# The first K product in two parts, the last combines spread over three engines, and other constants for the order of work

## The chip, the cores and the metric

One core of one Trainium2 chip. The metric is the device time in microseconds (us). A span (the time on the core itself, without what comes before and after) was shorter than the time of the same run (705.4 us of span went with 707.33 us).

## The reference, cut to what matters

```python
x = A_x                                       # 1 x 2048 x 512, bf16
g = sigmoid((x * gate_w).sum(-1, keepdims=True))
a = softmax(q k^T * 16**-0.5) v @ wo          # 32 heads of 16, q, k, v = x @ wqkv
b = ((x @ w_gate) * (x @ w_up)) @ w_down      # 512 -> 1376 -> 512
out = g * a + (1 - g) * b
```

## The kernel before

The program is a list of instructions that a small scheduler in the kernel file makes before anything runs. It keeps one clock for each engine with estimated durations, and always lets the engine whose clock is lowest take its next step. What comes out is a fixed order for each engine; on the chip the engines only wait on semaphores. So a changed constant gives another order for all that follows.

The score tiles (128 keys x 512 queries) go to two engines. ScalarE evaluates the exponential for 1508 tiles, two or three at a time. VectorE and GpSimd take the others through an integer form. The tensor engine fills the rest of its time with "fillers": the q, k, v, gate, up and down products, in `start_fill` and `do_fill`. A run of up to four score tiles takes one row group of the array for each tile, all at once. A pack is four matmuls of a filler or of the PV product (the exponentials times v) that go side by side in four column groups (four of the kernel before start together at 24.58 us and take 0.39). A bank is a 128 x 512 f32 piece of psS, psX or psO, the kernel's PSUM tensors, to which the tensor engine's results go.

The start, cut: the first 512 tokens of x are transposed, then Q and K of the first head group are made.

```python
def evac(bk, last):                       # of a K filler
    dst = KE[:, b, ch * 512 : (ch + 1) * 512]
    if b == ch == 0:                      # the first K product: two copies on ScalarE
        ev_k[0, 0, 0] = add("act", [last], lambda a: a.activation(dst[:, 0:128], bk.ap[:, 0:128], ACT.Copy), ...)
        ev_k[b, ch]   = add("act", [last], lambda a: a.activation(dst[:, 128:512], bk.ap[:, 128:512], ACT.Copy), ...)
        return
    ev_k[b, ch] = add("dve", [last], lambda v: v.tensor_copy(dst, bk.ap), 0.6, prio=2, ...)
# ...
for f, bk in ((f_q(0, 0, 0), slots[1][2]), (f_k(0, 0, 0), slots[0][2])):
    fills.append(f)
    start_fill(f, bk)
    # ...
    while st["fill"] is not None:
        do_fill(clock["pe"])
```

The x of the other three quarters comes by transposing loads, four each, all on SyncE's queue:

```python
for ch in range(1, NCH):
    for kt in range(KD):
        o = load("sp", xT[:, kt, ch * 512 : (ch + 1) * 512], x2[...], f"dx{ch}", 1.31, 3.5, transpose=True)
    d_x.append(o)
```

The tail, cut: the denominators of the last heads go through Ln and Exp on ScalarE by 128 tokens, VectorE multiplies, the tensor engine makes the last part of the output product, and VectorE combines `g * a + (1 - g) * b`.

```python
for tt in range(4):
    a1 = now("act", [dens[tt], free], ... ACT.Ln ...)
    a2 = now("act", [a1], ... ACT.Exp, scale=-1.0 ...)
    if tt == 2:
        fin(0)                                  # combine of tokens 0..127, then its store
    mt = now("dve", [a2] + ..., ... psO[:, cs] * rlast[:, cs] ...)
    oo.append(pe_tail([mt], last_pack, PACK, 0.44))
for tt in range(1, 4):
    fin(tt)
```

The softmax here doesn't subtract the row's maximum and nothing guards it: scores larger than these inputs give would overflow.

## Time and profile before

| | |
|---|---|
| Time, median of the first three runs | 707.34 us (706.64 to 708.81) |
| Span of the profiled run | 705.4 us |
| Busy: PE, ScalarE, VectorE, GpSimd | 682.9, 691.7, 651.9, 499.6 us |
| Exponentials on ScalarE | 670: 500 of two banks, 169 of three, 1 of one |
| First exponential, end of the last | 9.56, 696.11 us |

A row in order of time reads: start, duration, engine, line, operation, output<-input, shapes, count, and in brackets the idle time of the engine before it with what ended it. When rows are merged, the duration is from the start of the first to the end of the last. The prediction below shows the lines.

### The profile page before, as it was taken

To read this page: it belongs to the slowest core of one execution; us is meant where nothing else is said; L and a number is where in the kernel's file an instruction comes from. 1 tells how busy PE (TensorE), PEld (TensorE's weight loads), DVE (VectorE), ACT (ScalarE), POOL (GpSimd) and SP (SyncE) were. 2 spreads that over 40 slices of the span, in tenths; PEclk is the share of its full clock that TensorE was granted. 3 is DMA by queue.
4 is the path that set the end of the run, shared out by engine and by line. 5 is a ranking of instruction groups with operands and counts; after the bars stand their busy time and mean duration, and the time that the engine had idled before them with its cause. 6 is when DMAs were issued, how large, how long until landed. Compare 5 with 4: busy or idle time off the path is not lost.

```text
span 705.4 us, 21702 instructions
## 1 busy us (share of the span) xinstructions
PE 682.9 (97%) x9299; PEld 193.8 (27%) x9299; DVE 651.9 (92%) x1223; ACT 691.7 (98%) x685; POOL 499.6 (71%) x515
## 2 busy tenths in 40 slices
PE   8999999999999999999999999999999999999997
PEld 3323332222222222222222222222222222222222
DVE  5999999999999999999998999999999999998897
ACT  6999999999999999999999999999999999999995
POOL 4777786678867756678788756668888676664873
PEclk9999999999999999999999999999999999999999
DMA  7700001000300001000000011000000010000001
GB/s 142 260 13 8 21 18 22 18 17 7 98 21 17 18 12 36 29 17 18 20 3 27 18 34 35 18 7 16 21 18 18 13 34 28 17 19 20 3 21 46
DMA packets 33056, 21.67 MB, mean 31 GB/s; under 512 B 20380, under 2 KB 27964, under 8 KB 32960
## 3 DMA queue, kind: packets, MB, share of 16 engines
q1 hardware_dynamic: 31632, 19.64, 9.7%
q8 instruction: 72, 1.18, 0.7%
q10 hardware_dynamic: 1328, 0.66, 0.4%
q14 instruction: 24, 0.20, 0.1%
HBM read 15.12 MB, written 2.36 MB: 25 GB/s over the span
## 4 chain that ended last, share of the span: by engine, by line
ACT 71%; PE 22%; DVE 4%; issue 2%; POOL 0%; DVEq 0%; ACTq 0%; POOLq 0%
ACT PT L1744 55%; PE psS L503 7%; ACT xT L1744 7%; PE psO L1245 6%; ACT wv L1744 5%; PE psX L582 5%; ACT wd L1744 2%; ACT hT L1744 2%; PE psS L582 1%; PE psX L503 1%; DVE PT L1102 1%; PE psS L693 1%; PE psX L693 1%; PE psO L1852 0%; DVE PT L1180 0%
## 5 line engine op out<-in xcount | busy, mean ns | idle before, releaser
L1744 ACT ACTIVATE PT<-psS 128x1024 bf16<-128x1024 f32 (+1 forms) x502 | 568.1, 1428 | 0.1
L503 PE MATMUL psS<-QM,KE 32*128 32x512 bf16 x1974 | 254.7, 377 | 12.0 <-ACT PT L1744 6.1
L1183 POOL TENSOR_SCALAR PT<-PT 128x1024 int16<-128x1024 int16 x183 | 198.4, 1094 | 82.3 <-DVE PT L1102 31.8
L1245 PE MATMUL psO<-PT,VS 128*18 128x512 bf16 x1500 | 217.2, 381 | 0.9 <-DVE oraw L1274 0.9
L1102 DVE TENSOR_SCALAR PT<-psS 128x512 int16<-128x512 f32 x292 | 197.4, 684 | 14.0 <-PE psS L503 11.7
L1245 PE MATMUL psO<-PT,VD 128*18 128x512 bf16 x994 | 170.5, 381 | 0.0
L1043 PEld LDWEIGHTS <-KE 32*128 32x128 bf16 x2048 | 62.6, 91 | 274.5 <-issue 157.6
L1744 ACT ACTIVATE xT<-psS 128x1024 bf16<-128x1024 f32 (+2 forms) x56 | 72.8, 1338 | 0.0
L1180 DVE TENSOR_SCALAR PT<-PT 128x1024 int16<-128x1024 int16 x141 | 66.9, 491 | 0.8 <-PE psO L1245 0.2
L1183 POOL TENSOR_SCALAR PT<-xT 128x1024 int16<-128x1024 int16 x46 | 50.3, 1099 | 24.0 <-DVE xT L1102 7.9
L1744 ACT ACTIVATE wv<-psS 128x1024 bf16<-128x1024 f32 (+1 forms) x52 | 67.0, 1288 | 0.1
L1245 PEld LDWEIGHTS psO<-PT,VS 128*18 128x18 bf16 x1500 | 50.2, 88 | 51.3 <-issue 31.8
L1102 DVE TENSOR_SCALAR xT<-psS 128x512 int16<-128x512 f32 x76 | 51.6, 686 | 6.2 <-PE psS L503 5.9
L582 PE MATMUL psX<-wd,hT 128*32 128x512 bf16 (+3 forms) x784 | 55.9, 362 | 0.0
L582 PE MATMUL psX<-xT,wu 128*32 128x512 bf16 (+1 forms) x708 | 55.1, 378 | 0.3 <-DVE ost L917 0.3
L582 PE MATMUL psX<-xT,wg 128*32 128x512 bf16 (+1 forms) x696 | 54.3, 381 | 0.4 <-DVE KE L621 0.4
L1245 PE MATMUL psO<-xT,VS 128*18 128x512 bf16 x203 | 51.4, 381 | 0.7 <-DVE oraw L1274 0.4
L1245 PE MATMUL psO<-xT,VD 128*18 128x512 bf16 x242 | 51.1, 380 | 0.1
L1744 ACT ACTIVATE wd<-psS 128x1024 bf16<-128x1024 f32 (+1 forms) x40 | 47.6, 1316 | 0.0
L1245 PEld LDWEIGHTS psO<-PT,VD 128*18 128x18 bf16 x994 | 39.5, 88 | 26.3 <-issue 19.5
L1183 POOL TENSOR_SCALAR PT<-wv 128x1024 int16<-128x1024 int16 x34 | 36.8, 1089 | 9.1 <-DVE PT L1180 2.8
L1102 DVE TENSOR_SCALAR PT<-psX 128x512 int16<-128x512 f32 x52 | 35.7, 686 | 6.1 <-PE psS L503 5.5
(149 smaller groups left out, 1044.7 us busy)
## 6 DMA issues: line engine op xcount, KB each, us to landing
rb<-rscr SPq DMA_DIRECT2D x31, 256.0 KB
out_dram<-ost SPq DMA_DIRECT2D x12, 128.0 KB, 1.7
wu<-in_B_w_up_dram SPq DMA_DIRECT2D x1, 1376.0 KB, 8.7
wg<-in_B_w_gate_dram SPq DMA_DIRECT2D x1, 1376.0 KB, 11.5
wd<-in_B_w_down_dram SPq DMA_DIRECT2D x1, 1280.0 KB, 6.2
OT<-OX SPq DMA_DIRECT2D x60, 16.0 KB, 1.8
wo<-in_A_wo_dram SPq DMA_DIRECT2D x1, 512.0 KB, 12.3
out_dram<-wk SPq DMA_DIRECT2D x4, 128.0 KB, 1.7
```

What stands on the lines that cost most here:

```text
L503: return e.add_instruction(mybir.InstMatmult(name=nc.get_next_instruction_name(), engine=mybir.EngineType.PE, ins=[e.lower_ap(rhs), e.lowe ...
L582: return e.matmul(out_ap[32 * q : 32 * q + w, :], lhs[:, 32 * q : 32 * q + w], rhs, start=s0, stop=s1, tile_position=(0, 32 * q), skip_gro ...
L693: r = e.matmul(bk.ap[32 * q : 32 * q + 32, t2 * 256 : (t2 + 1) * 256], xT[:, kt, t * 128 + 32 * q : t * 128 + 32 * q + 32], wv[:, kt, bp * ...
L1043: r = e.ldweights(w, tile_position=pos)
L1102: lambda v: v.tensor_scalar(cell_ap(pr["cell"][i : i + 1], mybir.dt.int16), bk.ap, CB, 0.0, ALU.add, ALU.max),
L1180: fn = lambda v: v.tensor_single_scalar(cell_ap(c, I16), cell_ap(src, I16), 32.0 * k, ALU.add)
L1183: fn = lambda g: g.tensor_scalar(cell_ap(c, I16), cell_ap(src, I16), 32.0 * k, 1.0, ALU.add, ALU.mult)
L1245: r = e.matmul(psO[32 * j : 32 * j + VW, :], pv_stationary(m, kt, j, k), cell_ap((cell,)), start=s0, stop=s1, tile_position=(0, 32 * j), s ...
L1744: lambda a: a.activation(cell_ap(c), src, ACT.Exp, scale=LN2 / 128.0),
```

## The change

Its intent: let the first scores start as soon as the first 128 tokens of K are there, free VectorE of one combine at the end, and adjust the constants of the order. The core of the diff, cuts marked:

```diff
-        FP = 3
+        FP = 0                      # priority of the fillers' evictions on VectorE
+        KBE = "dve"
 ...
-                if b == ch == 0:    # the two ScalarE copies of one bank go
+        def f_k0(lo, hi, occ, eng, key, name):   # K of tokens lo..hi, in its own bank
 ...
+                    # second half of masked Q: not before the 384 part is copied
+                    alloc=None if p == 0 or c or b or KBE != "dve" else lambda t: None if ev_k.get((0, 0)) is None or ev_k[0, 0].end is None else [],
 ...
-   (f_q(0, 0, 0), slots[1][2]), (f_k(0, 0, 0), slots[0][2])
+   (f_q(0, 0, 0), slots[1][2]), (f_k0(0, 128, 0.11, "act", (0, 0, 0), "kA"), X), (f_k0(128, 512, 0.17, KBE, (0, 0), "k00"), slots[0][2])
 ...
-        K3L = 190 / K3H = 260 / WP = 28.0 / F1 = 1460.0 / SEED = 2 / KW = 4.5 / NFD = 24 / lat=5.5
+        K3L = 180.0 / K3H = 245.0 / WP = 46.0 / F1 = 1490.0 / SEED = 7 / KW = 4.0 / NFD = 20 / lat=5.1
 ...
+        def part0():                # combine of tokens 0..127: ScalarE, then GpSimd
+            k0 = now("act", ..., lambda a: a.activation(tmp, tailb[0].ap, ACT.Copy, scale=gval[:, t : t + 1]), 0.48, lat=0.7)
+            return now("pool", [k0, ev_b[c, 0]], lambda g: g.tensor_tensor(wk[:, 0, :], tmp, b_ap(t), ALU.add), 1.25)
 ...
+        for tt in range(3):
+            lnexp(tt)
+            mult(tt)
+        lnexp(3)
+        k1 = part0()
+        mult(3)
+        fin(1)
+        fin(2)
+        out0(k1)                    # its store, on SyncE, ahead of that of fin(3)
+        fin(3)
```

The diff also has half packs for the PV product, switched off by `HPV = 0`; with that the code is inert.

More of the change, by code (lines that the diff above doesn't have):

```diff
@@ L489, in _build @@
         HP = 1
+        HPV = 0
+        HN = [0, 0]
         HPK = 0.112
+        KBE = "dve"
         HTL = 0.04
@@ L608, in evac @@
                 dst = KE[:, b, ch * 512 : (ch + 1) * 512]
-                if b == ch == 0:
-                    bk.need += 1
-                    ev_k[0, 0, 0] = add(
-                        "act", [last], lambda a: a.activation(dst[:, 0:128], bk.ap[:, 0:128], ACT.Copy), 0.17, lat=0.38, cb=lambda k: bk.readers.append(k)
-                    )
-                    ev_k[b, ch] = add(
-                        "act", [last], lambda a: a.activation(dst[:, 128:512], bk.ap[:, 128:512], ACT.Copy), 0.38, lat=0.58, cb=lambda k: bk.readers.append(k)
-                    )
-                    return
                 ev_k[b, ch] = add(
@@ L627, in f_k, with evac @@
             return Fill(f"k{b}{ch}", packs, lambda: [d_wk[b]] + xdep(ch), evac, pos)
+        def f_k0(lo, hi, occ, eng, key, name):
+            packs = [
+                (
+                    lambda bk, kt=kt: col(bk.ap[:, lo:hi], wk[:, kt, 0:128], xT[:, kt, lo:hi], kt == 0, kt == KD - 1),
+                    occ,
+                    "c",
+                )
+                for kt in range(KD)
+            ]
+            def evac(bk, last):
+                bk.need += 1
+                src, dst = bk.ap[:, lo:hi], KE[:, 0, lo:hi]
+                if eng == "act":
+                    fn = lambda a: a.activation(dst, src, ACT.Copy)
+                else:
+                    fn = lambda v: v.tensor_copy(dst, src)
+                ev_k[key] = add(
+                    eng,
+                    [last],
+                    fn,
+                    0.06 + (hi - lo) / 960.0,
+                    prio=0,
+                    lat=0.25 + (hi - lo) / 960.0,
+                    cb=lambda k: bk.readers.append(k),
+                )
+            return Fill(name, packs, lambda: [d_wk[0]] + xdep(0), evac, -1)
         def f_q(c, b, pos):
@@ L1014, in _build @@
         first_pv = {}
-        pvst = {"m": 0, "oe": {}}
+        pvst = {"m": 0, "oe": {}, "half": None}
         o_mult = {}
@@ L1206, in pv_ready @@
         def pv_ready(t, partial=False):
+            if pvst["half"] is not None:
+                return pvst["half"][0]
             m = pvst["m"]
@@ L1221, in _build, with do_pv @@
         DB = slots[0][2]
-        def do_pv(got, t):
+        def do_pv(got, t, half=False):
+            if pvst["half"] is not None:
+                got, k0, deps, specs = pvst["half"]
+                pvst["half"] = None
+                return pv_mm(got, deps, specs, t, 1)
             m = pvst["m"]
@@ L1239, in do_pv, with pv_mm @@
                 specs.append((j, kt, k, cell, s0, first_pv[m, j] == need_pv[m, j]))
-                pv_left[m] -= 1
+                if not half:
+                    pv_left[m] -= 1
+            if half:
+                pvst["half"] = (got, None, deps, specs)
+                HN[1] += 1
+                return pv_mm(got, deps, specs, t, 0)
+            return pv_mm(got, deps, specs, t)
+        def pv_mm(got, deps, specs, t, half=None):
+            m = pvst["m"]
+            lastq = m == NM - 1
+            hs = slice(0, 512) if half is None else slice(256 * half, 256 * half + 256)
+            if half == 1:
+                pv_left[m] -= len(specs)
             def fn(e):
@@ L1245, in fn @@
                     r = e.matmul(
-                        psO[32 * j : 32 * j + VW, :],
+                        psO[32 * j : 32 * j + VW, hs],
                         pv_stationary(m, kt, j, k),
-                        cell_ap((cell,)),
+                        cell_ap((cell,))[:, hs],
                         start=s0,
@@ L1254, in fn @@
                 return r
-            kk = pe_run(deps, fn, PACK, "c", t)
+            kk = pe_run(deps, fn, PACK if half is None else HPK, "c", t)
+            if half == 0:
+                return kk
             for j, kt, k, cell, s0, s1 in specs:
@@ L1296, in norm @@
             bc = bass.AP(scs.tensor, scs.offset, [[512, 4], [0, 32], [1, 512]])
-            d = add("sp", [w], lambda e: e.dma_start(rb[:, s, :], bc), 0.1, lat=5.5, stream=f"drb{s}", dma=True)
+            d = add("sp", [w], lambda e: e.dma_start(rb[:, s, :], bc), 0.1, lat=5.1, stream=f"drb{s}", dma=True)
             g = NB * c + b
@@ L1341, in _build @@
         GP = 190.0
-        K3L = 190
-        K3H = 260
+        K3L = 180.0
+        K3H = 245.0
         B1, B2L, B2, B3L, B3 = 40.0, 100.0, 180.0, 200.0, 270.0
@@ L1353, in _build @@
         F0 = 220.0
-        WP = 28.0
+        WP = 46.0
         WL = 18.0
-        F1 = 1460.0
+        F1 = 1490.0
         fills.append(f_gate(GP))
@@ L1384, in _build @@
                 fills.append(f_q(c + 1, b, UA0[NQ * c + 2 * b + 2] + 30.0))
-        SEED = 2
+        SEED = 7
         for i, f in enumerate(fills):
@@ L1478, in _build @@
         PK = 2
-        KW = 4.5
+        KW = 4.0
         LAP = 0.08
@@ L1498, in _build @@
         SWE = 0
-        NFD = 24
+        NFD = 20
         AOH = 0.0635
@@ L1548, in convert @@
             st["na"] += 1
-        HN = [0]
         def half_pack(t, lim):
             f = st["fill"]
-            if f is None or f.name[0] not in "kqudw" + ("g" if f.name != "gate" else "") or t + HPK > lim or not HP or st["ua"] < 20:
+            if t + HPK > lim or not HP or st["ua"] < 20:
                 return False
+            if f is None or f.name == "gate" or f.name[0] == "v" or (HPV and pvst["half"] is not None):
+                pv = pv_ready(t) if HPV else None
+                if pv is None:
+                    return False
+                do_pv(pv, t, pvst["half"] is None)
+                return True
             do_fill(t, not f.h)
@@ L1880, in _build @@
         xt_all += [o_xt[-1 - kt] for kt in range(KD)]
-        for f, bk in ((f_q(0, 0, 0), slots[1][2]), (f_k(0, 0, 0), slots[0][2])):
+        for f, bk in ((f_q(0, 0, 0), slots[1][2]), (f_k0(0, 128, 0.11, "act", (0, 0, 0), "kA"), X), (f_k0(128, 512, 0.17, KBE, (0, 0), "k00"), slots[0][2])):
             fills.append(f)
@@ L1954, in _build @@
             cs = slice(tt * 128, (tt + 1) * 128)
-            pe_tail([hs[tt], o_sel] + old[tt], col(dbs[tt].ap[:, cs], sel, hi[:, cs], True, False), 0.06, 0.3)
-            dens.append(pe_tail([ls[tt]], col(dbs[tt].ap[:, cs], sel, lo[:, cs], False, True), 0.06, 0.3))
+            pe_tail([hs[tt], o_sel] + old[tt], col(dbs[tt].ap[:, cs], sel, hi[:, cs], True, False), 0.06, 0.24)
+            dens.append(pe_tail([ls[tt]], col(dbs[tt].ap[:, cs], sel, lo[:, cs], False, True), 0.06, 0.24))
         dens[2] = dens[3]
@@ L1965, in fin @@
                         clock[e_] += 0.02
-        for tt in range(4):
+        def part0():
+            t = 4 * c
+            tmp = oraw[:, 1 - s, :]
+            k0 = now(
+                "act",
+                [oo[0], ogate["g"], o_mult[NM - 2]],
+                lambda a: a.activation(tmp, tailb[0].ap, ACT.Copy, scale=gval[:, t : t + 1]),
+                0.48,
+                lat=0.7,
+            )
+            return now("pool", [k0, ev_b[c, 0]], lambda g: g.tensor_tensor(wk[:, 0, :], tmp, b_ap(t), ALU.add), 1.25)
@@ L1968, in _build, with out0, last_pack @@
+        def out0(k1):
+            t = 4 * c
+            o_out[t] = now(
+                "sp", [k1], lambda e: e.dma_start(out2[t * 128 : (t + 1) * 128, :], wk[:, 0, :]), 0.1, lat=2.0, stream=f"dout{t % 2}", dma=True
+            )
+        def last_pack(tt):
             cs = slice(tt * 128, (tt + 1) * 128)
-            a1 = now("act", [dens[tt], free], lambda a, tt=tt, cs=cs: a.activation(lnd[:, cs], dbs[tt].ap[:, cs], ACT.Ln), 0.29)
-            a2 = now("act", [a1], lambda a, cs=cs: a.activation(rlast[:, cs], lnd[:, cs], ACT.Exp, scale=-1.0), 0.22)
@@ L1971, in _build, with mult @@
-            if tt == 2:
-                fin(0)
+            return lambda e: col(tailb[tt].ap, OX[:, (NB - 1) % 2, cs], woz[:, 1, :], False, True)(e)
+        def mult(tt):
+            cs = slice(tt * 128, (tt + 1) * 128)
             mt = now(
                 "dve",
-                [a2] + oxfree.get((NB - 1) % 2, []),
-                lambda v, cs=cs: v.tensor_tensor(OX[:, (NB - 1) % 2, cs], psO[:, cs], rlast[:, cs], ALU.mult),
-                0.2,
-            )
-            def last_pack(e, tt=tt, cs=cs):
-                return col(tailb[tt].ap, OX[:, (NB - 1) % 2, cs], woz[:, 1, :], False, True)(e)
+                [a2s[tt]] + oxfree.get((NB - 1) % 2, []),
+                lambda v: v.tensor_tensor(OX[:, (NB - 1) % 2, cs], psO[:, cs], rlast[:, cs], ALU.mult),
+                0.2,
+            )
@@ L1982, in _build, with lnexp @@
             while len(half) <= tt:
-                assert tail_step(1e9)
-            oo.append(pe_tail([mt], last_pack, PACK, 0.44))
-        for tt in range(1, 4):
-            fin(tt)
+                if not tail_step(1e9):
+                    clock["pe"] += 0.02
+                    if qs["dve"] and not gen_step("dve"):
+                        clock["dve"] += 0.02
+            oo.append(pe_tail([mt], last_pack(tt), PACK, 0.44))
+        a2s = []
+        def lnexp(tt):
+            cs = slice(tt * 128, (tt + 1) * 128)
+            a1 = now("act", [dens[tt], free], lambda a: a.activation(lnd[:, cs], dbs[tt].ap[:, cs], ACT.Ln), 0.29, lat=0.24)
+            a2s.append(now("act", [a1], lambda a: a.activation(rlast[:, cs], lnd[:, cs], ACT.Exp, scale=-1.0), 0.22, lat=0.28))
@@ L1987, in _build @@
+        for tt in range(3):
[8 more added lines that the diff above has]
+        fin(3)
         _build.end = max(clock.values())
-        _build.hn = HN[0]
-        now("sp", [o_out[T - 1], o_out[T - 2]], lambda e: e.nop(), 0.1)
+        _build.hn = HN
+        now("sp", [o_out[T - 1], o_out[T - 2], o_out[T - 4]], lambda e: e.nop(), 0.1)
         _build.log = (P, conv)
```

## The prediction

> **What bounds the kernel now.** I read the page first (busy shares, slices, chain), then the busy time by stage, then the ScalarE rows by shape, and last the first 10 us and the last 9 us in order of time. The page:
>
> ```profile
> PE 682.9 (97%) x9299; PEld 193.8 (27%) x9299; DVE 651.9 (92%) x1223; ACT 691.7 (98%) x685; POOL 499.6 (71%) x515
> ACT  6999999999999999999999999999999999999995
> ...
> ACT 71%; PE 22%; DVE 4%; issue 2%; POOL 0%; DVEq 0%; ACTq 0%; POOLq 0%
> ...
> L1744 ACT ACTIVATE PT<-psS 128x1024 bf16<-128x1024 f32 (+1 forms) x502 | 568.1, 1428 | 0.1
> ```
>
> ScalarE is full in every slice but the first and the last, and the chain of waits is 71% ScalarE, almost all of it the softmax exponentials of line 1744. Three engines stand above 90%, so there is no idle engine to give its work to. The busy time by stage says where ScalarE is not full:
>
> ```profile
> 0.00:9.56 9.56, 7.86 (x62) 3.53 (x66) 2.99 (x12) 3.34 (x6) 2.11 (x9) 1.00 0.94 178
> 9.56:24.70 15.14, 14.85 (x281) 6.22 (x276) 13.55 (x23) 15.09 (x17) 10.20 (x27) 1.00 0.69 152
> 150.00:300.00 150.00, 146.82 (x1974) 40.44 (x1966) 141.45 (x262) 150.00 (x147) 110.17 (x102) 1.00 0.10 30
> 696.10:705.40 9.30, 5.07 (x116) 2.42 (x105) 5.38 (x16) 2.04 (x9) 0.89 (x1) 0.90 0.17 58
> ```
>
> Columns: stretch, its length, then busy us (and instructions) of PE, weight load, DVE, ACT, POOL, then clock, DMA share, GB/s. ScalarE has 9.56 us of lead-in, a body of 686.5 us, and 9.3 us of tail. ScalarE "busy" hides gaps, because the rows overlap: an exponential is recorded as 1.27 us but the next starts 0.90 us later.
>
> ```profile
> 34.65 1.27 ACT L1744 ACTIVATE hT<-psS 128x1024 bf16<-128x1024 f32 x1
> 35.55 1.28 ACT L1744 ACTIVATE PT<-psS 128x1024 bf16<-128x1024 f32 x1
> 36.45 1.29 ACT L1744 ACTIVATE hT<-psS 128x1024 bf16<-128x1024 f32 x1
> ```
>
> In the rows split by shape there are 500 exponentials of two banks, 169 of three and one of one bank. Where one stands alone, the start-to-start time is 0.90 to 0.93 us (mean 0.912) for two banks and 1.33 to 1.35 (mean 1.336) for three. So the bare work is 500 x 0.912 + 169 x 1.336 + about 0.8 = 682.6 us, and of the body's 686.5 only some 4 us are gaps. That is all that a better order of the body can win; the work itself (500 x 2 + 169 x 3 + 1 = 1508 tiles of 128x512) the change leaves alone.
>
> The start, in order of time:
>
> ```profile
> 7.62 1.03 PE L582 MATMUL psS<-xT,wk 128*32 128x512 bf16 x16
> 7.85 1.41 DVE L669 TENSOR_SCALAR QM<-psS,mask 128x512 bf16<-128x512 f32 x2 [1.43 <-PE psS L582]
> 8.71 0.28 ACT L612 ACTIVATE KE<-psS 128x128 bf16<-128x128 f32 x1 [1.69 <-PE psS L582]
> 8.88 0.48 ACT L615 ACTIVATE KE<-psS 128x384 bf16<-128x384 f32 x1
> ...
> 9.13 0.37 PE L503 MATMUL psX<-QM,KE 32*128 32x512 bf16 x1 [0.48 <-ACT KE L612]
> ...
> 9.56 2.85 ACT L1744 ACTIVATE hT<-psS 128x1024 bf16<-128x1024 f32 x3 [0.19 <-PE psS L503]
> 12.29 2.88 ACT L1744 ACTIVATE wd<-psS 128x1024 bf16<-128x1024 f32 x3
> 15.21 9.70 ACT L1744 ACTIVATE PT<-psS 128x1024 bf16<-128x1024 f32 x10
> ```
>
> The whole K product (16 matmuls of 512) must end before ScalarE copies the first 128 tokens; then the first scores, then the first exponential at 9.56. And the tail:
>
> ```profile
> 699.74 0.75 DVE L917 SCALAR_TENSOR_TENSOR wk<-psX,gval,wq 128x512 bf16<-128x512 f32 x1 [0.24 <-PE psX L582]
> 699.88 0.31 ACT L1970 ACTIVATE rb<-oraw 128x128 f32<-128x128 f32 x1
> 700.41 0.48 DVE L1976 TENSOR_TENSOR OX<-psO,rb 128x128 bf16<-128x128 f32 x2
> 700.52 2.70 SPq L926 DMA_DIRECT2D out_dram<-wk  x4
> 700.81 2.06 DVE L917 SCALAR_TENSOR_TENSOR wk<-psS,gval,wq 128x512 bf16<-128x512 f32 x3
> ```
>
> The first combine sits on VectorE between its second and third small multiply, and the last three combines follow.
>
> [...] the GpSimd add beside them should keep the 1.345 us that its 128x512 multiply (line 1306) has here.
>
> **The change, part by part.**
>
> *Start.* The K product becomes 4 packs of 128 columns into one bank, then 4 of 384 into another. The body's packs of 512 step by about 0.213 us (the four K packs: 7.62 to 8.65, less 0.18 of drain). A 128-column pack should be limited by its four weight loads, about 0.10 us (the row "0.75 for 16" has its waits in it): 4 x 0.11 = 0.44 us, so it ends at 7.62 + 0.44 + 0.18 = 8.24. ScalarE copies at 8.30 to 8.58 instead of 8.71 to 8.99. The first half of the masked Q is ready at 7.85 + 0.75 = 8.60. But the 384 part goes into PE's queue ahead of the scores: 4 x 0.165 = 0.66, so PE is free at 8.06 + 0.66 = 8.72. [...] scores start at about 8.83 instead of 9.13. First exponential near 9.26: gain 0.3. ScalarE loses the 384 copy, which cost it nothing (it waited). VectorE takes it (about 0.55 us, 8.95 to 9.5) and pushes the second half of masked Q behind it; VectorE had 0.74 us free before 10.99.
>
> What survives: exponentials 4 to 6 take 2.92 us against 3 x 0.905, and the ten from 15.21 take 9.49 against 9.05. So about 0.6 us of ScalarE gaps follow in the first 25 us, where the stage also has 69% DMA share. The next K chunk comes at its own pace there, from transposing loads. An earlier start runs sooner into that. I count half: 0.15 us.
>
> *Tail.* Moving the first combine off VectorE lets the third multiply start when its reciprocal is ready (9.38 + 0.31 after 690: 699.72) and the fourth at 700.22. The three combines then begin at about 700.45 instead of 700.81: 0.36 earlier. ScalarE's copy starts after the last exponential, 700.2[...]; GpSimd adds from 700.95 to 702.3; its store is issued at 702.35 and takes the queue about 0.3 us (four issues, last at 702.9, in the row of 2.70). The last combine ends at 700.45 + 2.06 = 702.51, so its store is issued at 702.65, not 702.55, and two stores of 128 KB are in flight together. I take 0.2 us of the 0.36.
>
> *Retuned order.* The change also alters constants of the program's own order of work: evictions of filler products at top priority on VectorE, 4.0 for 4.5 us of patience with GpSimd copies, other positions for the fillers, another seed. The half packs of the PV product are written but switched off, and the test that guards the old half packs keeps its meaning. None adds an instruction of note; they reshuffle the order, and with it the 4 us of gaps and the count of three-bank exponentials. Two three-bank exponentials in place of three two-bank ones save 3 x 0.912 - 2 x 1.336 = 0.064 us; twenty more or fewer of the 169 would be ten such exchanges, 0.64 us either way. Someone who retunes keeps what is better, so I lean to a gain: 0.6 us, uncertain by about 1.2.
>
> Sum: 0.15 + 0.2 + 0.6 = 0.95 us. 707.34 - 0.95 = 706.4; I say 706.3.
>
> **The rivals.** *A: the start's gain is lost.* K for the next 512 tokens or a busy bank (Q's bank now waits for the late second half) takes the place of the wait. For it: the 0.6 us of gaps named. Against: most of it comes at exponentials 4 to 7. It would make 706.5. *B: the store queue gives back the tail.* For: both late stores fall within 0.2 us. Against: the trace's stores land in 1.7 us while three are close together. 706.5 to 706.6; a GpSimd add of 1.6 us would even cost 0.2. *C: VectorE becomes the bound.* At 92% busy, it takes one more K eviction and, with less patience, more copies from GpSimd; ten more of 0.48 us are 4.8 us of its 53 idle ones, but at top priority filler evictions delay score evictions, and ScalarE would wait. That gives 708 to 709. *D: the reorder closes half the gaps*: 4 us to 2, 705.
>
> **Range and chances.** Start and tail together can hardly give more than 0.7 us or less than -0.2. The reorder spreads about 1.2 either way, and the three runs of before spread from 706.64 to 708.81, so a median has some 0.5 of its own. I take 704.7 to 707.7. Two per cent is 14 us, and the gaps, lead-in and tail that any of this touches are 4, 0.4 and 0.4 us: faster 0.005, slower 0.01, within 0.985.
>
> **What would show it.** Right: first exponential at 9.2 to 9.35, first K copy at about 8.3; the third multiply at about 699.7 measured from the same end of PV, with no combine between; [...] a GpSimd row of 1.3 us in the tail, last exponential to end 9.0 to 9.2 us instead of 9.3; body 685 to 687 us with 1508 tiles. Wrong: if scores still start after 9.05 (128-column packs cost as much as full ones); if the end hangs on the GpSimd row's store; if the body moves by over 2 us, which I can't work out from this profile, since it hangs on the order alone.

The sum is the printed one, 0.15 + 0.2 + 0.6 = 0.95 us, which takes 707.34 to 706.4. In the start, the step from 8.72 to 8.83 us is a term for going from packs to a run of scores: with it the start gains 0.3 us, of which half is counted; without it the same sum gives 0.4. (What the profile of the kernel before shows is that a run of scores starts 0.38 us after the pack ahead of it, 24.58 to 24.96, and a pack 0.22 after a pack, 25.27 to 25.49.) In the tail the duration of ScalarE's copy is cut, and its row among the signs at the end; the 700.95 us at which GpSimd's add starts rests on it, and so does the time of that part's store, one of the reasons to take 0.2 of the 0.36. The 0.36 itself does not. That the two parts of K need banks of their own, that the moved combine needs two instructions, and that VectorE's combines would not slow the GpSimd add, were my premises, and nothing then showed them.

Where the text gives a figure without its row, the profile of the kernel before has: four weight loads 0.11 us (twelve in 0.34, at 11.85); the 0.18 of "drain", a pack's record of 0.39 from 699.09 us less the 0.21 to the next pack at 699.30; VectorE's copies out of psS, psX and psO, 0.28 us for 128 columns and 0.68 for 512, between which the 0.55 for 384 lies. The 1.345 us is the mean of 16 GpSimd multiplies; the "them" beside which the add runs are VectorE's last combines.

## The result, and the profile after

| first session | before | changed |
|---|---|---|
| Time, median of 4 | 708.08 us (706.64 to 709.27) | 707.06 us (706.49 to 707.36) |
| Ratio (95% interval) | | 0.9986 (0.9963 to 1.0008) |
| Span of the profiled run | 705.4 us | 705.0 us |

A ratio is the mean time of one kernel's runs over that of the other's of the same rounds, so it is not quite the ratio of the medians. The page of the changed kernel:

```profile
PE 685.2 (97%) x9306; PEld 193.2 (27%) x9306; DVE 649.8 (92%) x1226; ACT 691.8 (98%) x687; POOL 495.6 (70%) x516
...
ACT 68%; PE 24%; DVE 4%; issue 3%; POOL 1%; DVEq 0%; ACTq 0%; POOLq 0%
...
L1794 ACT ACTIVATE PT<-psS 128x1024 bf16<-128x1024 f32 (+1 forms) x530 | 587.5, 1439 | 0.0
```

Nothing of the whole has moved: ScalarE is as full, and the chain is a little more on PE. The first 9 us in order of time:

```profile
6.97 0.43 PEld L585 LDWEIGHTS psX<-xT,wk 128*32 128x32 bf16 x16
7.19 0.39 PE L585 MATMUL psX<-xT,wk 128*32 128x128 bf16 x16
7.41 0.82 PE L585 MATMUL psS<-xT,wk 128*32 128x384 bf16 x16
7.42 0.75 DVE L692 TENSOR_SCALAR QM<-psS,mask 128x512 bf16<-128x512 f32 x1 [1.13 <-PE psS L585]
7.64 0.28 ACT L637 ACTIVATE KE<-psX 128x128 bf16<-128x128 f32 x1 [0.75 <-PE psX L585]
8.22 0.38 PE L506 MATMUL psX<-QM,KE 32*128 32x512 bf16 x1
8.65 1.02 ACT L1794 ACTIVATE hT<-psS 128x1024 bf16<-128x1024 f32 x1 [0.74 <-PE psS L506]
```

The first exponential is 0.91 us earlier (8.65 against 9.56). Only part of that is the change's: the first K matmul itself starts 0.43 us earlier, at 7.19 against 7.62, and nothing ahead of it was changed. From the first K matmul to the first exponential it is 1.46 us, against 1.94: a gain of 0.48. The 128-column packs cost PE only 7.41 - 7.19 = 0.22 us, because their weight loads had begun at 6.97, under the last pack of Q. K's copy ends at 7.92, and what scores wait for now is the masked Q, ready at 8.17.

Five microseconds later, ScalarE waits:

```profile
12.90 1.27 PE L717 MATMUL psS<-wv,xT 128*32 128x256 bf16 x40
12.91 0.68 DVE L615 CAST KE<-psX 128x512 bf16<-128x512 f32 x1
...
14.11 0.38 PE L506 MATMUL psX<-QM,KE 32*128 32x512 bf16 x1
...
14.54 1.02 ACT L1794 ACTIVATE hT<-psS 128x1024 bf16<-128x1024 f32 x1 [0.77 <-PE psS L506]
```

ScalarE has taken 11 of its 12 tiles of the first 512 keys. The second 512 keys of K are copied at 13.59, but the order that the scheduler fixed has 40 V matmuls of 256 columns (ten groups of four, to 14.17) ahead of the next scores. The tail:

```profile
699.69 0.67 ACT L2023 ACTIVATE oraw<-psX,gval 128x512 f32<-128x512 f32 x1
...
700.02 2.06 DVE L941 SCALAR_TENSOR_TENSOR wk<-psS,gval,wq 128x512 bf16<-128x512 f32 x3
...
700.43 1.15 POOL L2027 TENSOR_TENSOR wk<-oraw,wq 128x512 bf16<-128x512 f32 x1 [3.45 <-ACT oraw L2023]
700.79 1.08 SPq L950 DMA_DIRECT2D out_dram<-wk  x2
701.92 0.43 SPq L2032 DMA_DIRECT2D out_dram<-wk  x1
702.39 0.45 SPq L950 DMA_DIRECT2D out_dram<-wk  x1
```

VectorE's last combine ends at 702.08. But the queue issues the GpSimd part's store from 701.92 to 702.35, so the last store is issued at 702.39, when its data had been there for 0.31 us.

From here on I cut each profiled run at the same points, read from the single rows of each trace (in v_later below no exponential starts at just 17 or 47 tiles, and the value is interpolated): K is the start of the first K matmul; then the first exponential; the time at which 17 and 47 tiles have gone to ScalarE; the end of the last exponential; the tail's first cast (a copy to another type) on VectorE, which waits for the last PV product; the end of the last store's issue; the end of the span. For the two kernels, in us:

| | K at | K to first exp. | K to tile 17 | K to tile 47 | tile 47 to last exp. end | to first cast | to last store issued | to end | K to end |
|---|---|---|---|---|---|---|---|---|---|
| before | 7.62 | 1.94 | 9.84 | 23.41 | 665.09 | 0.74 | 6.37 | 2.13 | 697.74 |
| changed | 7.19 | 1.46 | 10.08 | 23.63 | 664.89 | 0.75 | 6.39 | 2.14 | 697.79 |

The start's 0.48 us is gone by tile 17 and is then a loss of 0.24. The tail's issue end is where it was. The body is 0.2 us shorter. From the first K matmul on, the two profiled kernels differ by 0.05 us.

### The profile page after: what moved, and what is told of

Read it like the earlier page. It is cut to its first block, busy times and chain, and to the rows that moved or that the text cites. A ratio compares the mean times of both kernels' runs of the same rounds, so it can differ in the third digit from the quotient of the medians.

```text
span 705.0 us, 21763 instructions
## 1 busy us (share of the span) xinstructions
PE 685.2 (97%) x9306; PEld 193.2 (27%) x9306; DVE 649.8 (92%) x1226; ACT 691.8 (98%) x687; POOL 495.6 (70%) x516
## 4 chain that ended last, share of the span: by engine, by line
ACT 68%; PE 24%; DVE 4%; issue 3%; POOL 1%; DVEq 0%; ACTq 0%; POOLq 0%
ACT PT L1794 56%; PE psS L506 8%; PE psO L1288 7%; PE psX L585 6%; ACT xT L1794 4%; ACT wv L1794 3%; ACT wd L1794 3%; ACT hT L1794 2%; DVE PT L1126 1%; PE psS L717 1%; PE psX L506 1%; PE psS L585 1%; POOL PT L1207 1%; PE psO L1902 0%; DVE wd L1126 0%
## 5 line engine op out<-in xcount | busy, mean ns | idle before, releaser
L1794 ACT ACTIVATE PT<-psS 128x1024 bf16<-128x1024 f32 (+1 forms) x530 | 587.5, 1439 | 0.0
L1207 POOL TENSOR_SCALAR PT<-PT 128x1024 int16<-128x1024 int16 x201 | 215.9, 1084 | 91.5 <-DVE PT L1126 30.2
L1204 DVE TENSOR_SCALAR PT<-PT 128x1024 int16<-128x1024 int16 (+1 forms) x143 | 68.6, 497 | 0.7
L1794 ACT ACTIVATE xT<-psS 128x1024 bf16<-128x1024 f32 (+1 forms) x51 | 66.0, 1367 | 0.0
L1794 ACT ACTIVATE wv<-psS 128x1024 bf16<-128x1024 f32 (+1 forms) x40 | 54.5, 1362 | 0.0
L1207 POOL TENSOR_SCALAR PT<-xT 128x1024 int16<-128x1024 int16 x34 | 36.9, 1091 | 23.5 <-PE psS L506 7.1
L1126 DVE TENSOR_SCALAR xT<-psS 128x512 int16<-128x512 f32 x62 | 42.3, 687 | 4.6 <-PE psS L506 3.9
L1207 POOL TENSOR_SCALAR xT<-PT 128x1024 int16<-128x1024 int16 x33 | 35.2, 1068 | 11.6 <-PE psO L1288 7.2
L1288 PE MATMUL psO<-xT,VS 128*18 128x512 bf16 x176 | 39.6, 381 | 0.4 <-ACT xT L1794 0.4
L1794 ACT ACTIVATE wd<-psS 128x1024 bf16<-128x1024 f32 (+1 forms) x30 | 39.5, 1407 | 0.0
```

Source lines behind the costliest of these rows:

```text
L1126: lambda v: v.tensor_scalar(cell_ap(pr["cell"][i : i + 1], mybir.dt.int16), bk.ap, CB, 0.0, ALU.add, ALU.max),
L1204: fn = lambda v: v.tensor_single_scalar(cell_ap(c, I16), cell_ap(src, I16), 32.0 * k, ALU.add)
L1207: fn = lambda g: g.tensor_scalar(cell_ap(c, I16), cell_ap(src, I16), 32.0 * k, 1.0, ALU.add, ALU.mult)
L1288: r = e.matmul(psO[32 * j : 32 * j + VW, hs], pv_stationary(m, kt, j, k), cell_ap((cell,))[:, hs], start=s0, stop=s1, tile_position=(0, 32 ...
L1794: lambda a: a.activation(cell_ap(c), src, ACT.Exp, scale=LN2 / 128.0),
```

## The experiments

The theory after this reading: the gain at the start is lost at the 12th tile, the gain on VectorE's tail is given back in the store queue, and the constants do little. The rival is my prediction: a small gain in each part.

### The three parts by themselves

`tail_only` is the kernel before with the new tail, `start_only` with the split K product and the delayed half of Q, `knobs_only` with the constants. The edit of each is that part of the diff above, for example:

```diff
 # start_only: against the kernel before
-   (f_k(0, 0, 0), slots[0][2])
+   (f_k0(0, 128, 0.11, "act", (0, 0, 0), "kA"), X), (f_k0(128, 512, 0.17, KBE, (0, 0), "k00"), slots[0][2])
 # knobs_only: FP, K3L, K3H, WP, F1, SEED, KW, NFD and the one latency; tail_only: from pe_tail's latency on
```

What was expected of tail_only: 

> The kernel before with only the new tail (first of the last four combines on ScalarE and GpSimd, new order of the tail's steps). Theory (the gain on VectorE is given back by the store queue): VectorE's last combine ends about 0.38 us earlier after the last exponential than in the kernel before (there 702.87 - 696.11 = 6.76 us, here 6.4), but the last store's issue ends at the same distance (7.1 us) because the GpSimd part's store is issued just ahead of it; last exponential to end of span 9.3 +- 0.1 us, body the same order as before, time within 0.3 us of before. Rival (the tail's 0.36 us is won, and the body lost it in the changed kernel): last exponential to end 8.9 to 9.0, time 0.3 to 0.4 us less than before.

Of start_only: 

> The kernel before with only the split K product and the delayed second half of masked Q; all constants of the order and the tail as before. Theory: from the first K matmul to the first exponential 1.46 us instead of 1.94 (gain 0.48)[...]; K's next 512 tokens are ready earlier too, so 36 tiles are through about 0.5 to 0.7 us sooner, and the time is 0.3 to 0.8 us less than before, if the body keeps its length. Rival A (the gain is lost at the next K chunk): 36 tiles are through no sooner than 16.9 + 9.3 us, time within 0.2 of before. Rival (reordered body is random): the body from first to last exponential differs from 686.55 us by over 0.5 either way.

Of knobs_only: 

> The kernel before with only the changed constants of the order of work (priority of filler evictions, patience, positions, seed, a latency). Theory: it makes nothing or a small loss: body from first to last exponential 686.5 to 687.5 us, time -0.3 to +1.0 us against before. Rival (my prediction): body 0.6 us shorter than 686.55, time about 0.6 us less.

Of after_again, the changed kernel once more: 

> The changed kernel again, on the same chip as the three parts. Theory: the parts add up: time against before is the sum of the three parts' differences within 0.6 us; first K matmul to first exponential 1.46 us again, but the first K matmul itself may start anywhere from 7.2 to 7.7 us[...]: then 0.3 to 0.4 us of the 0.91 us by which the first exponential came earlier is not the change's. Rival: the first K matmul starts at 7.2 in all runs of the changed kernel and at 7.6 in all with the old start.

Measured, five rounds on one chip (before: 707.05 us median of 9):

| run | median | ratio to before (95%) | exponentials | K at | K to first exp. | K to tile 17 | K to tile 47 | tile 47 to last exp. | to first cast | to store issued | K to end |
|---|---|---|---|---|---|---|---|---|---|---|---|
| tail_only | 706.71 | 1.0000 (0.9987 to 1.0013) | 670 | 7.38 | 1.94 | 9.85 | 24.10 | 664.95 | 0.74 | 6.30 | 698.26 |
| start_only | 707.52 | 1.0008 (0.9995 to 1.0020) | 674 | 7.48 | 1.46 | 10.08 | 23.63 | 665.21 | 1.67 | 6.12 | 698.59 |
| knobs_only | 707.05 | 0.9998 (0.9985 to 1.0010) | 665 | 6.72 | 1.95 | 9.85 | 23.44 | 664.46 | 1.36 | 6.37 | 697.61 |
| after_again | 706.99 | 0.9996 (0.9983 to 1.0010) | 672 | 6.75 | 1.47 | 10.11 | 25.01 | 664.78 | 0.75 | 6.36 | 699.05 |

What follows. *The tail alone* is no gain: the last store's issue ends 6.30 us after the first cast, against 6.37. From the last exponential it is 703.47 - 696.43 = 7.04, where I expected 7.1, and to the end of the span 9.21, inside the expected 9.3 +- 0.1.

*The start* gives its 0.48 us every time and loses it every time: tile 17 is through at 10.08, with the old start at 9.85, to 0.03 in all of these runs. My expectation that 36 or 47 tiles would be through 0.5 to 0.7 us sooner was wrong, and so was the hoped-for lower time: start_only is the slowest of the four. It also has more left after its last exponential, 1.67 us to the first cast. The rival that the reordered body is random names over 0.5 us of change from first to last exponential; it was 0.83 (687.38), but 0.7 of that is the start's own gain and loss.

*The constants* with the old start shorten the body by 0.6 us, as I had predicted (664.46 against 665.09) and had then given up in my expectation; but they leave 0.6 us more between the last exponential and the last PV product (1.36 against 0.74), so nothing remains.

*No part and no sum is clear of noise* in the times, which is what all four intervals say. The record also lists each run's span, and by these start_only is worse: 705.92 us on average of five runs, against 705.03 of nine of the kernel before. That fits the profiles, 698.59 against 697.74 from K to the end. The medians of the parts differ from before by -0.34, +0.47 and 0.00 us, the whole by -0.06, so they add up within the 0.6 us that was expected, which is no sharp test.

The repeat shows where part of the noise sits. The first K matmul started at 6.75 us in one profile of the changed kernel and at 7.19 in the other, and anywhere from 6.64 to 7.62 in the fourteen profiles of this study, with the old start and the new. (I had expected 7.2 to 7.7, which was too narrow; the rival, that the start decides it, is out.) The matmuls before it differ as well. The first transpose starts within 0.23 us in all fourteen (4.18 to 4.41), but the transposes of x have a median of 314 ns in the first profiles of both kernels and of 219 in after_again and knobs_only, where K started at 6.75 and 6.72; the matmuls of Q, of 512 columns in both kernels, have 515 ns in the profile of before and 379 in these two. In the profiles of before, the changed kernel, tail_only and after_again the seven matmuls of 512 columns that stand ahead of the transposes take 3.17 us, with starts 0.43 us apart, where the later packs of 512 step by 0.213. Why the moment differs from run to run isn't shown: the column of the granted clock shows 1.00 all through the first 9 us, in the profiles of before and of the changed kernel alike.

And after_again has a stall that the other profile has not, 1.38 us between tile 25 and tile 27:

```profile
21.95 0.40 PE L585 MATMUL psX<-xT,wk 128*32 128x512 bf16 x4 [1.38 <-DMA xT<-in_A_x_dram]
...
22.71 1.02 ACT L1794 ACTIVATE PT<-psS 128x1024 bf16<-128x1024 f32 x1 [1.16 <-PE psS L506]
```

The tensor engine's order has the K product of the last quarter of x there, and its transposing loads landed at 21.82 us. Each of the twelve takes 1.26 us of SyncE to issue, but one or two in each profile take 1.6 to 2.9. The last quarter landed anywhere from 20.18 to 21.88 us. Leave out one_bank and v_later below, whose order differs there. In the five other profiles where it landed over 13.9 us after the first K matmul, tile 47 came 0.38 to 1.38 us late; in the seven where it landed within 13.6 us, it did not (23.41 to 23.44 us after K with the old start, 23.63 with the new). So an early start of K runs into a landing time that does not move with it. That is the form in which the prediction's rival A is real, beside the V products.

### The store on another queue, the two parts in one bank, the V products later, the old seed

```diff
 # act_store: against the changed kernel
-                "sp", [k1], lambda e: e.dma_start(out2[...], wk[:, 0, :]), ...
+                "act", [k1], lambda e: e.dma_start(out2[...], wk[:, 0, :]), ...
 # one_bank: the copy of the first part is put ahead of the second part, which then waits for it
-            ... "kA"), X), (f_k0(128, 512, 0.17, KBE, (0, 0), "k00"), slots[0][2])):
+            ... "kA"), X), (f_k0(128, 512, 0.17, KBE, (0, 0), "k00"), X)):
+            while f.name == "k00" and qs["act"]:
+                clock["act"] += 0.0 if act_step() else 0.02
 # v_later
-            fills.append(f_v(0, tg, 0))
+            fills.append(f_v(0, tg, 11.5 if tg else 0))
 # after_seed2
-        SEED = 7
+        SEED = 2
```

Expected of act_store: 

> The changed kernel, with the store of the GpSimd part issued on ScalarE's queue instead of SyncE's. Theory (the store queue gives the tail's gain back): the last store is issued as soon as VectorE's last combine ends, 0.25 to 0.35 us earlier; from the first copy out of the PV bank (first of the tail's VectorE casts) to the end of the span 8.2 to 8.3 us, against 8.54 before and 8.55 and 8.52 in the two profiles of the changed kernel. Rival (landing of the stores sets the end[...]): still 8.45 to 8.6.

Of one_bank: 

> The changed kernel, with both parts of the first K product in the same bank: the 384 part has to wait until ScalarE has copied the 128 out. Theory (the banks of their own are what lets the second part run during the copy): the wait adds about 0.6 us, so from the first K matmul to the first exponential about 2.0 to 2.2 us instead of 1.46, no better than the 1.94 of the kernel before. Rival (the short first part alone gives the gain): 1.45 to 1.6 us.

Of v_later: 

> The changed kernel, with the V fillers after the first one held back until 12 tiles have gone to ScalarE. Theory (the start's 0.48 us is lost at the 12th tile, because scores on the second 512 tokens of K stand behind ten V packs in the tensor queue, 12.90 to 14.17 us): the ScalarE gap there falls from 0.77 us to 0.2 to 0.5, and 17 tiles are through at most 9.8 us after the first K matmul, against 10.08 to 10.10 in the changed kernel and 9.85 before. Rival (K's second chunk itself comes late, by its transposing load or its copy on VectorE): the gap stays at 0.7 or more and 17 tiles take 10.0 us or more.

Of after_seed2: 

> The changed kernel with the old seed of the filler positions, nothing else. Theory (the retuned constants only draw another order from a narrow spread): from the exponential at tile 47 to the last exponential's end 663.3 to 664.8 us, against 664.2 before, 664.0 and 663.9 in the two profiles of the changed kernel, with another count of three-bank exponentials. Rival (the new seed is what makes the body short): over 665 us.

One look each (single runs, state unknown; the kernel before took 707.25 us beside them; all correct):

| run | time | exponentials | PE busy | K to first exp. | K to tile 17 | tile 47 to last exp. | to first cast | to store issued |
|---|---|---|---|---|---|---|---|---|
| act_store | 706.48 | 672 | 685.3 | 1.46 | 10.08 | 664.88 | 0.75 | 5.99 |
| one_bank | 715.20 | 676 | 687.0 | 1.98 | 10.69 | 667.84 | 3.79 | 7.71 |
| v_later | 734.28 | 708 | 706.4 | 1.47 | 9.60 | 674.47 | 17.32 | 6.92 |
| after_seed2 | 717.85 | 690 | 695.9 | 1.47 | 10.08 | 666.16 | 9.58 | 7.72 |

**act_store** shows the theory of the store queue right. The tail in order of time:

```profile
700.21 2.06 DVE L941 SCALAR_TENSOR_TENSOR wk<-psS,gval,wq 128x512 bf16<-128x512 f32 x3
...
700.98 1.65 SPq L950 DMA_DIRECT2D out_dram<-wk  x3
701.81 0.37 ACTq L2032 DMA_DIRECT2D out_dram<-wk  x1
```

The three VectorE combines' stores now follow their data; the last is issued by 702.63, 5.99 us after the first cast instead of 6.39. From the first cast to the end it is 8.26 us, inside the expected 8.2 to 8.3. (The expectation's 8.54, 8.55 and 8.52 for the other profiles are 8.50, 8.53 and 8.51 by the cut points of these tables.)

**one_bank** shows what it costs when both parts share a bank and the second waits for the copy:

```profile
7.10 0.28 ACT L637 ACTIVATE KE<-psX 128x128 bf16<-128x128 f32 x1 [0.91 <-PE psX L585]
7.43 0.83 PE L585 MATMUL psX<-xT,wk 128*32 128x384 bf16 x16 [0.38 <-ACT KE L637]
...
8.62 1.02 ACT L1794 ACTIVATE hT<-psS 128x1024 bf16<-128x1024 f32 x1 [1.25 <-PE psS L506]
```

The second part waits 0.38 us of PE for the copy, and the first exponential comes 1.98 us after K, no better than the 1.94 of before (expected: 2.0 to 2.2, missed by 0.02). Whether the second part would need that wait is not shown: no run here has the copy and the matmuls in one bank at the same time.

**v_later** shows that the V products are what makes ScalarE wait at the 12th tile. Without them the scores start as soon as K is copied:

```profile
13.85 0.38 PE L506 MATMUL psX<-QM,KE 32*128 32x512 bf16 x1 [0.78 <-DVE KE L615]
...
14.29 1.45 ACT L1794 ACTIVATE hT<-psS 128x1536 bf16<-128x1536 f32 x1 [0.31 <-PE psS L506]
```

The wait falls from 0.77 to 0.31 us, and tile 17 is through at 9.60, ahead of both kernels; both were expected so. The lead doesn't last: at the 27th tile ScalarE waits 0.72 us for scores, after the tensor engine has waited 1.20 us for the copy of a V product that now comes later. And the whole takes 734.28 us, 27 more.

That and **after_seed2** overturn the other half of my theory, that another order is drawn from a narrow spread. One constant of the changed kernel, a seed that shifts filler positions by up to six tiles, is worth 10.8 us (717.85 in one run against the median of 707.06, on another chip; against the kernel before beside it, 10.6). From tile 47 to the last exponential it takes 666.16 us; the expectation counts from one exponential later, 0.9 us, so its 663.3 to 664.8 are 664.2 to 665.7 here, and the rival's "over 665" is met. The run's first rows are those of the changed kernel to 0.1 us up to tile 47, and ScalarE's last exponential ends at 696.62, only 0.9 us later than in the changed kernel. The time is lost behind that. Here are the page's first line and the tensor engine after the last exponential:

```profile
PE 695.9 (97%) x9310; PEld 193.8 (27%) x9310; DVE 652.1 (91%) x1237; ACT 693.1 (97%) x705; POOL 486.4 (68%) x506
```

```profile
699.03 4.07 PE L585 MATMUL psS<-wd,hT 128*32 128x512 bf16 x72
702.92 2.55 PE L585 MATMUL psX<-wd,hT 128*32 128x512 bf16 x44
```

Of the down product 160 matmuls, so 40 packs of four or 8.5 us at 0.213, stand after the last exponential (116 of them in these two rows); in the changed kernel there are none. The tensor engine has 10.7 us more to do (695.9 - 685.2), with the same products and the same 2048 score tiles. What differs is how the tiles are grouped: 690 exponentials instead of 672, because more of them hold two tiles. Each group is a run of its own on the tensor engine: the matmul records show 672, 690 and, in v_later, 708 runs of scores. A run of two tiles takes as long as one of four (0.39 and 0.38 us in the rows), and by the program it changes the array from column to row groups and back. 10.7 us over 18 more groups is 0.59 us a group, and v_later gives 21.2 us over 36, which is 0.59 as well. Both are counted from the same profile, though, and PE times move by 1.4 us between two profiles of one kernel; between runs that differ by under ten groups the ratio scatters. The single records give a direct reading: in the changed kernel, from the start of the last pack before a run to the start of the first pack after it is 0.67 us on average, for runs of two tiles as for runs of three (four: 0.70), and between two packs it is 0.21. So a run adds some 0.46 us, short waits included. Of the 10.7 us that is about 8; what the rest is, isn't shown.

```profile
PE 706.4 (96%) x9334; PEld 198.1 (27%) x9334; DVE 657.8 (90%) x1229; ACT 697.3 (95%) x723; POOL 490.7 (67%) x508
```

So the kernel has two bounds at once. ScalarE's work is fixed, and the prediction saw that. The tensor engine has only some 20 us of idle time in 705, 14 of them in short gaps of the body and 6 in lead-in and tail. In after_seed2 it has as much, 20.1 us: the further groups weren't taken from its idle time, and what they cost came back as fillers at the end.

### The version with the moved store, one with the old start, and two more seeds

```diff
 # old_start_new_rest: act_store with the start of the kernel before
-   (f_k0(0, 128, ...), X), (f_k0(128, 512, ...), slots[0][2])
+   (f_k(0, 0, 0), slots[0][2])
 # before_seed7: the kernel before
-        SEED = 2
+        SEED = 7
 # after_seed3: the changed kernel
-        SEED = 7
+        SEED = 3
```

Expected of act_store_timed: 

> The changed kernel with the GpSimd part's store on ScalarE's queue, timed. Theory: the order of the body is the changed kernel's, so only the tail moves: first tail cast to end 8.2 to 8.3 us again, first K matmul to end of span 697.5 +- 0.2 us if no transposing load hiccups into the third K chunk (before 697.78, changed kernel 697.81), and the time 0.3 us below the kernel before, which five rounds will hardly tell from nothing: ratio 0.998 to 1.001. Rival: the tail is over 8.4 again.

Of old_start_new_rest: 

> The changed constants and the new tail with the store on ScalarE's queue, but the first K product whole, as in the kernel before. Theory (the split start costs 0.2 us net at the 12th tile and the constants with the old start save 0.6): body as in the run of the constants alone, 685.9 to 686.2 us; first K matmul to end of span 697.2 to 697.6; the time 0.2 to 0.6 us below the kernel before and not above that of the changed kernel with the moved store. Rival (the split start is worth its 0.48 us): the time is over that of the other by 0.3 or more.

Of before_seed7: 

> The kernel before with the new seed of the filler positions alone. Theory (every change of the order redraws how many score tiles go in one run; with fewer tiles a run the tensor engine falls behind and fillers are left after the last exponential, about 0.47 us for each exponential more): the time follows the count of exponentials: with 670 +- 5 of them 706 to 709 us, with 690 about 716, with 708 about 730. A draw worse than 708 is as likely as not. Rival (only the changed kernel is so fragile): 706 to 708.5 whatever the count.

Of after_seed3: 

> The changed kernel with a third seed. Theory: as for the last one, time follows the count of exponentials (672 in the changed kernel, 690 with the old seed at 717.85 us): 707 + 0.55 us for each exponential over 672, within 3 us; work left on the tensor engine after the last exponential, if there are over 680. Rival (the old seed was a freak): 706 to 708 us.

The 0.47 and 0.55 us for each exponential more are my estimates; the runs above give 0.46 by the matmul records and 0.59 by the PE times.

Measured; the first two in five rounds (before: 707.32 us median of 9), the others in one look:

| run | time | ratio to before (95%) | exponentials | PE busy | K to first exp. | K to tile 17 | K to tile 47 | tile 47 to last exp. | to first cast | to store issued | K to end |
|---|---|---|---|---|---|---|---|---|---|---|---|
| act_store_timed | 706.52 | 0.9985 (0.9972 to 0.9999) | 672 | 683.9 | 1.47 | 10.11 | 24.56 | 664.79 | 0.75 | 5.99 | 698.17 |
| old_start_new_rest | 706.79 | 0.9989 (0.9977 to 1.0002) | 665 | 678.8 | 1.94 | 9.84 | 24.28 | 664.34 | 1.36 | 5.99 | 697.85 |
| before_seed7 | 707.99 | | 677 | 685.3 | 1.94 | 9.85 | 23.41 | 665.17 | 1.04 | 7.22 | 698.97 |
| after_seed3 | 707.91 | | 670 | 683.2 | 1.48 | 10.09 | 24.01 | 665.52 | 1.45 | 6.32 | 699.44 |

The changed kernel with the store on ScalarE's queue is the only version whose interval leaves 1 out, if narrowly: 0.15% below the kernel before, about 1 us. Less than half of that lies in the spans: their mean is 704.80 us against 705.26, which is 0.46 us, close to the 0.4 us by which the tail's store issue ends sooner. The other 0.6 us lies outside the spans (1.62 us against 2.22), where no profile shows what it is. Its tail is 5.99 us again; from the first cast to the end it is 8.07, where 8.2 to 8.3 was expected. Its K to end missed the 697.5 that I expected, at 698.17; there the last quarter of x landed at 21.35 us, 14.6 after K, and tile 47 came 0.93 us late, which the expectation had excepted.

Whether the old start is better with the new rest is not settled by the times: 706.79 against 706.52 on the same chip, with intervals of 0.13% on each side. In the profiles it is ahead, 697.85 against 698.17 from K on, but both have the stall at the load (0.87 and 0.93 us), so the expected 697.2 to 697.6 was missed, and with it the body of 685.9 to 686.2 (686.68).

The two seeds did not come out as badly as the old one in the changed kernel. before_seed7 came at 707.99 with 677 exponentials (expected: 706 to 709 for 665 to 675, about 716 for 690) and after_seed3 at 707.91 with 670 (expected within 3 us of 707). Each is 0.6 to 0.7 us above the median of the kernel before, in a single run. So of three seeds not chosen for their kernel one is over 708, and by 10 us; three draws don't test my "as likely as not". Nor do the two new ones decide between theory and rival, since 707.99 and 707.91 lie in the rivals' ranges too (706 to 708.5, 706 to 708). The count of exponentials alone does not tell the time either. one_bank has 676, one less than before_seed7, and is 7 us slower. There the tensor engine did 20.08 us of work in its first 24.7 us, against 23.16 in the changed kernel, and 13 packs of the down product were left at the end. So it can be made late by waiting as well as by smaller groups; that this start is the whole cause of its 8 us is argued and not shown. Its trace also has the tensor engine wait 1.16 us for a transposing load, at 15.65 us.

## Why the prediction was right, and where its steps failed

The time lay in the range (707.06 in 704.7 to 707.7). The point was 0.76 us low, and the sum was not right for the right reasons: two of its three gains were given back, and that the time came out near is in part luck. Of the signs that the prediction names, the body just missed (687.05 us against 685 to 687), last exponential to end missed (9.28 against 9.0 to 9.2), and one of the signs of being wrong came true, the GpSimd part's store at the end. Point by point:

- **The bound.** Right as far as it went: ScalarE's work stayed (1508 tiles), its body moved by under a microsecond. It missed that PE bounds the end as well, through the number of groups.
- **Start, 0.3 us to the first exponential.** Too small: 0.48 from the first K matmul. The term that was mis-sized is "4 x 0.11 = 0.44 us" for the 128-column packs. The weight loads took 0.43 in all, as estimated, but they began under the last Q pack, and PE spent 0.22. The first scores wait for the masked Q at the end.
- **"I count half: 0.15 us."** Wrong: none survives, and 0.22 to 0.27 us are lost by tile 17. The place is right, the next K, but not the reason: the step that failed is that K comes late by its transposing loads. At the 12th tile K is there at 13.59 and the scores stand behind V products, as v_later shows (the wait falls from 0.77 to 0.31 us). A late landing, as the prediction has it, costs time only later, at tile 25, in five of the profiles.
- **Tail, 0.2 of 0.36 us.** VectorE gained as worked out (from the first cast to its last combine's end 5.63 us against 6.01; the third and fourth multiply start at 699.31 and 699.81, which with the 0.41 us by which this tail began sooner are the 699.72 and 700.22 of the prediction). All of it is given back, as rival B said: the last store's issue ends at 6.39 against 6.37. The mis-sized term is the issue of a store, taken as 0.3 and measured at 0.43 to 0.45 where two queue up (0.33 to 0.34 for each of the four in the kernel before). The ScalarE copy took 0.67 us (the estimate of it is cut) and the GpSimd add 1.15 (1.345 taken), beside VectorE's combines, so that no slowing by them shows. Its part was ready at 701.58; the queue was not.
- **Retuned order, 0.6 us.** Right for the old start (664.46 against 665.09, knobs_only), but paid for by a later last PV product, and 0.2 with the new start. What failed is the spread, "uncertain by about 1.2": a single seed moves the changed kernel by 10.8 us. So that the constants on hand do well isn't because orders differ little. Whether they suit this start better than the old one isn't shown: with the old start the times are the same within the noise (707.05 against 706.99 without the moved store, 706.79 against 706.52 with it).
- **Rival C**, VectorE as the bound: nothing of it. VectorE was busy 649.8 us against 651.9.
- **Rival D**: by the sum of the prediction, gaps are 4.65 us in the changed kernel (687.05 less 508 x 0.912 and 164 x 1.336) and 4.0 before, so none were closed; the 0.7 more are the wait at the 12th tile.

What the difference of the first session's medians (1.02 us) consists of can't be told from the profiles: from K to the end they differ by 0.05 us, and the second session's ratio is 0.9996. I take it for scatter, which is argued and not shown: the profiles have up to 0.98 us in the first K matmul's start and 1.38 us in a wait for the transposing loads, and the time outside the spans moves by a microsecond between runs of the kernel before.

## What to carry to other kernels

A gain at the start of a program with a fixed order has to be followed to the next shared arrival: here, to the next piece of K, where 0.7 us was lost, most of it to what stood ahead of the scores in the queue. Before an operation is moved to an idle engine, look at what its result needs next: a store issued in a shared queue ahead of the last one gave back all that the move had won (6.39 against 6.37 us from first cast to last store issued), and another queue kept it (5.99). And when two engines are full, count the groups that the second has to run, and hold the order's constants fixed, before any part of a change is credited with the time.
